# Larger first loads, a reordered start, respaced attention pieces, and the k softmax reciprocal on ScalarE instead of VectorE

## The chip, the cores and the metric

The kernel runs on one core of a Trainium2 chip. The metric is the device time of one execution in microseconds (us). Five engines work side by side, each in the order of its own queue: TensorE (PE, with its weight loads PEld), VectorE (DVE), ScalarE (ACT), GpSimd (POOL) and SyncE (SP, which here only issues transfers).

## The reference

A pre-layernorm block on x of 2048 x 640 (bf16): linear attention with a softmax feature map, then a GELU-gated feed-forward part.

```python
x = A_x
h  = x + A(_layernorm(x), wqkv, w_phi, wo)
h2 = h + (gelu(ln(h) @ w_gate) * (ln(h) @ w_up)) @ w_down        # F = 1536

def A(x, wqkv, w_phi, wo):                                        # 32 heads of 20
    q, k, v = split(x @ wqkv)
    pq, pk = q @ w_phi, k @ w_phi                                 # per head
    phi_q = concat(softmax(pq), softmax(-pq))
    phi_k = concat(softmax(pk), softmax(-pk))
    kv = phi_k^T v;   z = sum over s of phi_k
    o  = (phi_q kv) / (phi_q z + 1e-6)
    return o @ wo
```

## The kernel before

The 2048 rows are 16 tiles of 128 rows, in four blocks of four tiles. Every engine's order is the order of the code: the whole body runs under a manual schedule. SP, too, issues its transfers in code order, and waits at each one for what it reads.

**Start (lines 158 to 196 and 342 to 379).** x tiles 0 to 3 are loaded one by one, alternately from SP and ACT; then ACT loads w_phi, and SP loads Wv in five pieces, x tiles 4 to 7 in two, the transposed k weights WkT, x tiles 8 to 11, WqT, and x tiles 12 to 15. `ln_st` takes the statistics of a tile on DVE (two bn_stats, L106, and one bn_aggr, L108) and the reciprocal root on POOL (L110, L112); with `act=True` POOL also makes mr = -mean*rstd (L117), which `ln_ap` needs when it normalizes on ACT (L123). Otherwise `ln_ap` normalizes on DVE (L128). `ln_tp` transposes a normalized tile on PE into LN1T. `v_part` is a part of a v projection, ordered by weight chunk. `fold` multiplies the k (later q) weights with the block-diagonal feature map BD (L212; BD is built by DVE at L366), and ACT and DVE copy the results to Wk2 (later Wq2) in turn.

**The k loop (lines 384 to 423), one round per tile t.** PE projects k (`k_tile`, L248), ACT makes the two exponentials E of +pk and -pk (L280), PE projects v of tile t+4, ACT copies it to one of six buffers vS (L268). `ln_ap(t + 6)` normalizes a coming tile on ACT, and SP transposes it by a transfer (L139). In `k_norm` DVE sums E by head (L287), takes the reciprocal rs (L291), and v is scaled by it into vt (L295): the half for s = 1 on POOL, the half for s = 0 on DVE one round later, or on POOL for the tiles in VP. At odd t from 5 on, `kv_tile` adds tiles t-5 and t-4 to the kv sums in PSUM (L313). In the last round, t = 15, the first four groups of q (`q_mm`, 35 matmuls of 512 columns, and `q_exp`, their exponentials on ACT, L340) stand in the code between `k_tile(15)` and `k_norm(15)`; kv tiles 10 to 15 follow on PE.

**After the loop.** `kv_mask` brings the sums into the weight KV. PE then takes the rest of q between the attention pieces of tiles 0 and 1, and from there the feed-forward part runs in units: 12 `gate_up` (L556; GELU L559 on ACT, product L562 on DVE) and then `down` (L571). `weave` puts the attention pieces of later tiles ahead of units by hand-written offsets: `attn_a` (L451, L459), `attn_b`, `b2`, `b3` (L472 to L496, and the transposing transfer oT by SP), `attn_c` (L511), `attn_d` (L525), `attn_d2` (L532 to L539), `attn_e` (normalize on ACT, transposing transfer LN2T). Pieces that fall behind the last unit are carried over to the next `weave`. Block 0 is done in two weaves of 256 columns (tiles 0 and 1, then 2 and 3), with 12 gate_up and 4 down units each; the blocks after it are done with 512 columns, and a gate_up of block 1 reads LN2T of all of tiles 4 to 7.

Of the kernel before, what the change touches and what calls it, by code (L numbers as in the profile page):

```python
# [17 lines left out]
def kernel(  # L18
# [74 lines left out]
    def small(pool, shape, name, bufs=3):  # L93
        return pool.tile(shape, F32, name=name, bufs=bufs)
# [1 line left out]
    def gtile(name):  # L96
        return psG.tile([P, 2, 512], F32, name=name, tag="G")

    def ln_stats(pool, tiles, tag, act=True):

        n = len(tiles)
        mv = small(pool, [P, n, nc.vector.BN_AGGR_DIM], "mv" + tag)
        stats = small(pool, [P, n, 2, nc.vector.BN_STATS_DIM], "stats" + tag)
        for j, xt in enumerate(tiles):
            for i in range(2):
                nc.vector.bn_stats(stats[:, j, i, :], xt[:, i * HD:(i + 1) * HD])  # L106
        for j in range(n):
            nc.vector.bn_aggr(mv[:, j, :], stats[:, j])  # L108
        ve = small(pool, [P, n], "ve" + tag)
        nc.gpsimd.tensor_scalar_add(ve, mv[:, :, 1], EPS)  # L110
        rstd = small(pool, [P, n], "rstd" + tag)
        nc.gpsimd.tensor_tensor(rstd, ve, nhalf[:, 0:n], op=ALU.pow)  # L112

        mr = small(pool, [P, n], "mr" + tag)
        if act:
            for j in range(n):
                nc.gpsimd.tensor_scalar(mr[:, j:j + 1], mv[:, j, 0:1], rstd[:, j:j + 1], -1.0,  # L117
                                        op0=ALU.mult, op1=ALU.mult)
        return [(xt, mv[:, j, 0:1], rstd[:, j:j + 1], mr[:, j:j + 1]) for j, xt in enumerate(tiles)]
# [28 lines left out]
    Wk2 = p1.tile([P, NC, D], BF16, name="Wk2")  # L148
    acc = p1.tile([P, NC, 4, VC], F32, name="acc")

    vS = [p1.tile([P, H, VC], BF16, name=f"vS{i}") for i in range(6)]
    fp_cm = tc.tile_pool(name="fp", bufs=1, side="right", reuse_waits="tile")
    fp = fp_cm.__enter__()
    WkT = fp.tile([P, NC, D], BF16, name="WkT")
    WqT = p1.tile([P, NC, D], BF16, name="WqT")


    for t in range(4):
        (nc.sync, nc.scalar)[t % 2].dma_start(x_sb[0][:, t:t + 1, :], x_v[:, t:t + 1, :])
    nc.scalar.dma_start(wphi, phi_v.rearrange("(c p) f -> p c f", p=P))  # L160
    for c in range(NC):
        nc.sync.dma_start(Wv[:, c, :], w_v[:, c, 2 * D:3 * D])
    for t in (0, 2):
        nc.sync.dma_start(x_sb[1][:, t:t + 2, :], x_v[:, 4 + t:6 + t, :])
    nc.sync.dma_start_transpose(WkT, A_wqkv[:, D:2 * D])
    wo_v = A_wo.rearrange("(c p) n -> p c n", p=P)
    wg_v = B_w_gate.rearrange("(c p) n -> p c n", p=P)
# [3 lines left out]
    nc.sync.dma_start(x_sb[3], x_v[:, 12:16, :])  # L171


    nc.gpsimd.memset(nhalf, -0.5)

    ones = fp.tile([P, 2], F32, name="ones")
    nc.scalar.activation(ones, nhalf, ACTF.Exp)
    zero = fp.tile([P, 512], BF16, name="zero")
    nc.vector.memset(zero, 0.0)
    for i in range(6):  # L180
        nc.vector.memset(vS[i][:, :, Dh], 1.0)
    make_identity(nc, ident)
    nc.gpsimd.memset(hmask, 1.0)
# [40 lines left out]

    lnp, Ek, Vt = {}, {}, {}

    def ln_st(*tiles, act=True):
        for t, v in zip(tiles, ln_stats(p1, [x_sb[t // 4][:, t % 4, :] for t in tiles], "1", act)):
            lnp[t] = v

    def ln_ap(t, on_act=False, on_pe=False):
        ln = (ln_act if on_act else ln_dve)(p1, "1", *lnp[t])
        if on_pe:
            lnp[t] = ln
        else:
            transpose_to(LN1T[t // 4][:, :, t % 4 * P:(t % 4 + 1) * P], ln, False)

    def ln_tp(t, on_dve=False):
        transpose_to(LN1T[t // 4][:, :, t % 4 * P:(t % 4 + 1) * P], lnp[t], True, on_dve)
# [18 lines left out]
    def v_part(t, *cs):  # L258

        if 0 in cs:  # L260
            pv[t] = gtile("pv")
        for c in cs:
            for u in range(2):
                nc.tensor.matmul(pv[t][:, u, 0:HD], lhsT=lnT(t, c), rhs=Wv[:, c, u * HD:(u + 1) * HD],
                                 start=(c == 0), stop=(c == NC - 1))

    def v_ev(t):
        nc.scalar.copy(vS[t % 6][:, :, 0:Dh].rearrange("p (u h) f -> p u h f", u=2),  # L268
                       pv[t][:, :, 0:HD].rearrange("p u (h f) -> p u h f", f=Dh))

    def v_tile(t):
        v_mm(t)
        v_ev(t)

    def k_tile(t):
        pk = gtile("pk")
        proj(pk, t, Wk2)
        Ek[t] = ev.tile([P, 2, D], BF16, name="E", bufs=8)
        for s in range(2):
            nc.scalar.activation(Ek[t][:, s, :].rearrange("p (u f) -> p u f", u=2), pk[:, :, 0:HD],  # L280
                                 ACTF.Exp, scale=(1.0 if s == 0 else -1.0))

    def k_norm(t):


        sk = small(p1, [P, 2 * H], "sk")
        nc.vector.reduce_sum(sk, Ek[t].rearrange("p s (h f) -> p (s h) f", f=Dh), axis=AX.X)  # L287
        if t - 1 in todo:
            todo.pop(t - 1)()
        rs = small(p1, [P, 2 * H], "rs")  # L290
        nc.vector.reciprocal(rs, sk)  # L291
        Vt[t] = vt = ev.tile([P, 2, H, VC], BF16, name="vt", bufs=8)

        def mult(s, eng):
            eng.tensor_tensor(vt[:, s], vS[t % 6], rs[:, s * H:(s + 1) * H, None].to_broadcast([P, H, VC]), ALU.mult)  # L295

        mult(1, nc.gpsimd)
        if t in VP:
            mult(0, nc.gpsimd)
        elif t == NT - 1:  # L300
            mult(0, nc.vector)
        else:
            todo[t] = lambda: mult(0, nc.vector)

    todo = {}

    def kv_tile(t):

# [29 lines left out]
    def q_exp(j, signs=(0, 1)):  # L338
        for s in signs:
# [4 lines left out]
    ln_ap(0, on_pe=True)  # L344
    ln_tp(0)
    warm(WA)
    ln_ap(1, on_pe=True)
    ln_tp(1)
    warm(WB)
    ln_st(2, act=False)  # L350
    ln_st(3, act=False)
    ln_ap(2, on_pe=True)
    ln_ap(3, on_pe=True)
    v_part(0, 0, 1, 2)
    v_part(1, 0)
    v_part(0, 3)
    v_part(1, 1)
    ln_tp(2)
    v_part(0, 4)
    v_part(1, 2, 3)  # L360
    ln_tp(3)
    v_part(1, 4)
    v_ev(0)
    v_ev(1)

    nc.vector.tensor_tensor(BD, wphi[:, :, None, :].to_broadcast([P, NC, 8, Dh]),  # L366
                            hmask[:, :, :, None].to_broadcast([P, NC, 8, Dh]), ALU.mult)
    v_tile(2)
    ln_st(4, 5, act=False)
    ln_st(6)  # L370
    v_mm(3, (0,))
    fold(WkT, Wk2, False, (0, 1))
    ln_ap(4, on_pe=True)
# [2 lines left out]
    ln_ap(5, on_pe=True)  # L376
    fold(WkT, Wk2, False, (2, 3, 4))
    ln_tp(4, True)
    ln_st(7)
    fp_cm.__exit__(None, None, None)  # L380
    ev_cm = tc.tile_pool(name="ev", bufs=1, side="right", reuse_waits="tile")
    ev = ev_cm.__enter__()
# [1 line left out]
    for t in range(NT):  # L384
        if t == T3:
            ps_cm.close()
            psG = ps_cm.enter_context(tc.tile_pool(name="psG", bufs=3, space=PSUM, reuse_waits="tile"))
            psK = ps_cm.enter_context(tc.tile_pool(name="psK", bufs=1, space=PSUM, reuse_waits="tile"))
            kvp = psK.tile([P, 2, 512], F32, name="kvp")
        k_tile(t)  # L390
        if t == 0:
            ln_tp(5)
            ln_ap(6)
        if t in FQ:
            fold(WqT, Wq2, True, [i for i, f in enumerate(FQ) if f == t])
        for j in range(len(QT)):
            if t == QT[j]:
                q_mm(j)
                q_exp(j)
        if t + 4 < NT:  # L400
            v_tile(t + 4)
        if t > 0 and t + 6 < NT:
            ln_ap(t + 6, on_act=True)
        if t % 2 == 0 and t + 8 < NT:
            ln_st(t + 8, t + 9)
        k_norm(t)
        if t % 2 == 1 and t >= 5:
            kv_tile(t - 5)
            kv_tile(t - 4)
        if t == 9:  # L410
            nc.gpsimd.memset(KV, 0.0)
            nc.gpsimd.memset(kmask, 1.0)
            for r in HALF:
                nc.gpsimd.affine_select(out=kmask[r], in_=kmask[r], pattern=[[4, NC], [-Dh, 4]],
                                        compare_op=ALU.is_ge, fill=0.0, base=0, channel_multiplier=1)
                nc.gpsimd.affine_select(out=kmask[r], in_=kmask[r], pattern=[[-4, NC], [Dh, 4]],
                                        compare_op=ALU.is_ge, fill=0.0, base=Dh - 1, channel_multiplier=-1)
            nc.gpsimd.tensor_copy(KV[:, :, 0, :, KC - 1], kmask)
            nc.gpsimd.tensor_copy(KV[:, :, 1, :, 0], kmask)
        if t == 10:  # L420
            nc.sync.dma_start(Wg, wg_v)
            nc.sync.dma_start(Wo, wo_v)
            nc.sync.dma_start(Wu, wu_v)
# [181 lines left out]
    def gus(b, a0, a1):  # L605
        return [(gate_up, b, f, a0, a1) for f in range(NF)]
# [33 lines left out]
    attn_e(0, True, True)  # L640
    q_mm(q + 6)
    q_exp(q + 6)
    attn_ln(1, True)
    attn_e(1, True, True)
    attn_a(2, 2)
# [2 lines left out]
    def attn_at(t, i, offs):  # L648
# [2 lines left out]
        return [(i + o, fn, t) for fn, o in zip(fns, offs) if o >= 0]  # L651

    SHORT = (0, 2, 3, 4, 9, 9, 10, 12)
    LONG = (0, 1, 2, 3, 6, 6, 7, 8)


    weave(gus(0, 0, 256) + downs(0, (0, 1)),
          attn_at(2, 0, (-1, 0, 1, 2, 7, 7, 8, 10)) + attn_at(3, 1, SHORT) + attn_at(4, 6, SHORT) + attn_at(5, 9, SHORT) +
          attn_at(6, 13, SHORT))
    weave(gus(0, 256, 512) + downs(0, (2, 3)), attn_at(7, 2, SHORT))  # L660
    for b in range(1, NB):
        stages = []
        if b + 1 < NB:
# [34 lines left out]
```

The softmax here doesn't subtract the row's maximum and nothing guards it: scores larger than these inputs give would overflow.

## Time and profile before

| | us |
|---|---|
| median of 12 runs | 283.61 (283.44 to 284.79) |
| the profiled execution: time | 283.56 |
| its span in the profile | 281.8 |
| PE busy / DVE / ACT / POOL | 272.8 / 166.1 / 140.3 / 95.6 |
| first projection of v starts (PE) | 7.90 |
| first projection of k starts (PE) | 16.66 |
| q groups in round 15, first start (PE) | 62.09 |
| last kv sum ends (PE) | 72.22 |
| first gate_up of block 1 starts (PE) | 146.24 |

The profile gives all times in us from the span's start; the execution's own time is 1.76 us more than the span. "PE busy" counts overlapping matmuls once and is near to the span; where PE waits is read from the chain of waits and from the order of its instructions. The transposing transfers appear as instructions of SP (SPq) where they are issued, with their landing told apart.

### The profile page before, as it was taken

How to read it: one execution, taken by the hardware profiler on the slowest of the kernel's cores; microseconds unless marked ns; L12 is line 12 of the kernel's file. 1: busy time of each engine (PE TensorE's matmuls, PEld its weight loads, DVE VectorE, ACT ScalarE, POOL GpSimd, SP SyncE). 2: the span in 40 equal slices, each digit the busy share in tenths (PEclk: the TensorE clock that was granted, in tenths of full speed). 3: DMA queues.
4: the chain of work that ended last, by engine and by line, in shares of the span. 5: the costliest groups of instructions: out<-in, count | busy, mean ns of one | idle time of the engine just before them, and what ended most of it. 6: DMA issues, size and time to landing. Idle time of an engine off the chain costs nothing.

```text
span 281.8 us, 5752 instructions
## 1 busy us (share of the span) xinstructions
PE 272.8 (97%) x2326; PEld 171.5 (61%) x2326; DVE 166.1 (59%) x289; ACT 140.3 (50%) x226; POOL 95.6 (34%) x211
## 2 busy tenths in 40 slices
PE   7999999999999999999799999999999999999995
PEld 2677777764555777778564555675455567444573
DVE  4999998788496676667223848332566632333222
ACT  2679889678596855465334454412446350222200
POOL 6258987686102217436112234210135230000000
PEclk9999999999999999999999999999999999999999
DMA  7991332693520021322120113131031613000011
GB/s 223 256 267 29 72 45 53 181 392 129 185 99 0 3 47 34 84 49 59 38 68 4 23 27 70 25 95 47 2 47 23 70 27 93 26 0 1 0 49 47
DMA packets 40523, 21.05 MB, mean 75 GB/s; under 512 B 33200, under 2 KB 38704, under 8 KB 40496
## 3 DMA queue, kind: packets, MB, share of 16 engines
q1 hardware_dynamic: 39552, 20.32, 28.5%
q10 hardware_dynamic: 944, 0.35, 0.5%
q8 instruction: 18, 0.29, 0.5%
q14 instruction: 9, 0.07, 0.1%
HBM read 10.18 MB, written 2.62 MB: 45 GB/s over the span
## 4 chain that ended last, share of the span: by engine, by line
PE 86%; DVE 5%; ACT 3%; DMA 3%; POOL 1%; issue 1%; ACTq 0%; POOLq 0%
PE gu L556 35%; PE pd L571 18%; PE pq L335 8%; PE po L511 7%; PE pk L248 7%; PE pv L248 5%; PE kvp L313 2%; PE ab L451 2%; DVE stats L106 2%; DMA oT<-o 2%; DMA x_sb<-in_A_x_dram 1%; DVE sk L287 1%; ACT E L280 1%; ACT Eq L340 1%; PE wa L212 1%
## 5 line engine op out<-in xcount | busy, mean ns | idle before, releaser
L559 ACT ACTIVATE g<-gu 128x512 bf16<-128x512 f32 (+1 forms) x60 | 30.7, 512 | 75.2 <-PE gu L556 74.0
L562 DVE TENSOR_TENSOR GT<-gu,g 128x512 bf16<-128x512 f32 (+1 forms) x60 | 34.5, 581 | 54.2 <-ACT g L559 54.0
L556 PE MATMUL gu<-LN2T,Wg 128*128 128x512 bf16 (+1 forms) x300 | 61.8, 337 | 0.9 <-DVE GT L562 0.8
L556 PE MATMUL gu<-LN2T,Wu 128*128 128x512 bf16 (+1 forms) x300 | 61.7, 336 | 0.0
L571 PE MATMUL pd<-Wd,GT 128*128 128x320 bf16 x384 | 53.9, 299 | 0.0
L571 PEld LDWEIGHTS <-GT 128*128 128x128 bf16 x384 | 37.4, 98 | 15.7 <-DVE GT L562 0.9
L556 PEld LDWEIGHTS <-Wu 128*128 128x128 bf16 x300 | 29.3, 98 | 22.6
L556 PEld LDWEIGHTS <-Wg 128*128 128x128 bf16 x300 | 28.4, 98 | 21.7 <-issue 1.0
L248 PEld LDWEIGHTS <-LN1T 128*128 128x128 bf16 x300 | 28.5, 98 | 11.6 <-issue 0.7
L295 POOL TENSOR_TENSOR vt<-vS,rs 128x672 bf16<-128x672 bf16 x22 | 29.8, 1372 | 9.1 <-DVE rs L291 7.1
L577 DVE TENSOR_TENSOR y<-pd,x_sb 128x640 bf16<-128x640 f32 (+1 forms) x17 | 13.3, 784 | 30.7 <-PE pd L571 30.7
L459 ACT COPY AB<-ab 128x704 f32<-128x704 f32 x28 | 19.6, 748 | 14.4 <-PE ab L451 14.1
L511 PE MATMUL po<-Wo,oT 128*128 128x320 bf16 x160 | 24.4, 299 | 1.8 <-DMA oT<-o 1.8
L287 DVE TENSOR_REDUCE sk<-E 128x64 f32<-128x1280 bf16 x16 | 23.3, 1455 | 3.3 <-ACT E L280 3.3
L248 PE MATMUL pk<-Wk,LN1T 128*128 128x320 bf16 x160 | 24.1, 299 | 0.4 <-ACT E L280 0.3
L492 DVE TENSOR_TENSOR tt<-AB,w 128x1280 bf16<-128x1280 f32 x16 | 23.8, 1487 | 1.2 <-POOL w L485 0.9
L280 ACT ACTIVATE E<-pk 128x640 bf16<-128x640 f32 x32 | 20.8, 706 | 6.8 <-PE pk L248 6.6
L335 PE MATMUL pq<-LN1T,Wq 128*128 128x512 bf16 x100 | 22.9, 379 | 0.0
L248 PE MATMUL pv<-Wv,LN1T 128*128 128x320 bf16 x140 | 21.3, 299 | 0.0
L340 ACT ACTIVATE Eq<-pq 128x1024 bf16<-128x1024 f32 (+1 forms) x22 | 19.4, 950 | 3.7 <-PE pq L335 3.7
L511 PEld LDWEIGHTS <-oT 128*128 128x128 bf16 x160 | 15.5, 98 | 9.2 <-DMA oT<-o 2.2
L534 POOL TENSOR_SCALAR v<-sm 128x1 f32<-128x1 f32 x14 | 8.4, 599 | 32.0 <-DVE x_sb L525 32.0
(80 smaller groups left out, 262.5 us busy)
## 6 DMA issues: line engine op xcount, KB each, us to landing
out_dram<-y SPq DMA_DIRECT2D x15, 160.0 KB, 1.9
Wg<-in_B_w_gate_dram SPq DMA_DIRECT2D x1, 1920.0 KB, 7.5
Wu<-in_B_w_up_dram SPq DMA_DIRECT2D x1, 1920.0 KB, 14.9
Wd<-in_B_w_down_dram SPq DMA_DIRECT2D x1, 1920.0 KB, 7.8
x_sb<-in_A_x_dram SPq DMA_DIRECT2D x2, 640.0 KB, 4.7
Wv<-in_A_wqkv_dram SPq DMA_DIRECT2D x5, 160.0 KB, 3.9
Wo<-in_A_wo_dram SPq DMA_DIRECT2D x1, 800.0 KB, 9.1
x_sb<-in_A_x_dram SPq DMA_DIRECT2D x2, 320.0 KB, 4.7
```

Of the source, the lines that this page charges most:

```text
L248: nc.tensor.matmul(ps[:, u, 0:HD], lhsT=lnT(t, c), rhs=W[:, c, u * HD:(u + 1) * HD], start=(c == 0), stop=(c == NC - 1))
L280: nc.scalar.activation(Ek[t][:, s, :].rearrange("p (u f) -> p u f", u=2), pk[:, :, 0:HD], ACTF.Exp, scale=(1.0 if s == 0 else -1.0))
L287: nc.vector.reduce_sum(sk, Ek[t].rearrange("p s (h f) -> p (s h) f", f=Dh), axis=AX.X)
L295: eng.tensor_tensor(vt[:, s], vS[t % 6], rs[:, s * H:(s + 1) * H, None].to_broadcast([P, H, VC]), ALU.mult)
L335: nc.tensor.matmul(pqs[j][:, i, :], lhsT=Wq2[:, kc, c * P:(c + 1) * P], rhs=LN1T[b][:, kc, :], start=(kc == 0), stop=(kc == NC - 1))
L340: nc.scalar.activation(Eq[j][:, :, s, :], pqs[j][:, 0:len(QG[j])], ACTF.Exp, scale=(1.0, -1.0)[s])
L492: nc.vector.tensor_tensor(tt.rearrange("p s (h f) -> p s h f", f=Dh), num, w[:, :, :, None].to_broadcast([P, 2, H, Dh]), ALU.mult)
L511: nc.tensor.matmul(po[:, u, 0:HD], lhsT=st[t][:, c, :], rhs=Wo[:, c, u * HD:(u + 1) * HD], start=(c == 0), stop=(c == NC - 1))
L556: nc.tensor.matmul(gu[:, i, 0:n], lhsT=W[:, c, f * P:(f + 1) * P], rhs=LN2T[b][:, c, a0:a1], start=(c == 0), stop=(c == NC - 1))
L559: nc.scalar.activation(g[:, 0:n], gu[:, 0, 0:n], ACTF.Gelu_apprx_tanh)
L562: nc.vector.tensor_tensor(st[b, "g", f][:, a0:a1], gu[:, 1, 0:n], g[:, 0:n], ALU.mult)
L571: nc.tensor.matmul(pd[:, u, 0:HD], lhsT=st[b, "g", f][:, tl * P:(tl + 1) * P], rhs=Wd[:, f, u * HD:(u + 1) * HD], start=(f == 0), stop=(f ...
```

## The change

First loads: x tile 0 from SP, tile 1 from ACT, tiles 2 and 3 in one load from SP; Wv in three loads; of tiles 4 to 7 one half from SP, one from ACT. An explicit load of activation table set 6 replaces the small Exp that came first on ACT. Start: the normalizing of tile 1 goes between the two bn_stats of tile 2; BD is built ahead of the normalizing of tile 3; the v parts of tiles 0 and 1 stand in another order. k loop: `ln_ap(t + 6)` on DVE; E is summed in two halves; Ln and Exp(-x) on ACT (`k_rs`) give the reciprocal, one round later; `k_vt` makes both halves of vt after it; vS has seven buffers. In round 15 `k_rs(15)` and `k_vt(15)` follow at once. After the loop a small GELU stands behind the last q_exp. Attention pieces: from `attn_c` on, tiles 4 to 6 come one unit later; tile 7 starts one unit later, and its `attn_c` and the pieces after it come two later.

```diff
-    def ln_stats(pool, tiles, tag, act=True):
+    def ln_stats(pool, tiles, tag, act=True, between=None):
...
                 nc.vector.bn_stats(stats[:, j, i, :], xt[:, i * HD:(i + 1) * HD])
+                if between and i == j == 0:
+                    between()
...
-    for t in range(4):
-        (nc.sync, nc.scalar)[t % 2].dma_start(x_sb[0][:, t:t + 1, :], x_v[:, t:t + 1, :])
+    nc.gpsimd.memset(nhalf, -0.5)
+    nc.sync.dma_start(x_sb[0][:, 0:1, :], x_v[:, 0:1, :])
+    nc.scalar.dma_start(x_sb[0][:, 1:2, :], x_v[:, 1:2, :])
+    nc.sync.dma_start(x_sb[0][:, 2:4, :], x_v[:, 2:4, :])
+    for c0, c1 in ((0, 2), (2, 4), (4, 5)):
+        nc.sync.dma_start(Wv[:, c0:c1, :], w_v[:, c0:c1, 2 * D:3 * D])
+
+    nc.scalar.add_instruction(mybir.InstLoadActFuncSet(name=nc.get_next_instruction_name(), act_func_set_id=6))
     nc.scalar.dma_start(wphi, phi_v.rearrange("(c p) f -> p c f", p=P))
-    for c in range(NC):
-        nc.sync.dma_start(Wv[:, c, :], w_v[:, c, 2 * D:3 * D])
-    for t in (0, 2):
-        nc.sync.dma_start(x_sb[1][:, t:t + 2, :], x_v[:, 4 + t:6 + t, :])
+    nc.sync.dma_start(x_sb[1][:, 0:2, :], x_v[:, 4:6, :])
+    nc.scalar.dma_start(x_sb[1][:, 2:4, :], x_v[:, 6:8, :])
     nc.sync.dma_start_transpose(WkT, A_wqkv[:, D:2 * D])
...
-    nc.gpsimd.memset(nhalf, -0.5)
-
-    ones = fp.tile([P, 2], F32, name="ones")
-    nc.scalar.activation(ones, nhalf, ACTF.Exp)
...
-    for i in range(6):
+    for i in range(7):
         nc.vector.memset(vS[i][:, :, Dh], 1.0)
...
             nc.scalar.activation(Ek[t][:, s, :].rearrange("p (u f) -> p u f", u=2), pk[:, :, 0:HD],
                                  ACTF.Exp, scale=(1.0 if s == 0 else -1.0))
+        if t > 0:
+            k_rs(t - 1)
+
+    def k_rs(t):
+
+        sk = st1[t]
+        nc.scalar.activation(sk, sk, ACTF.Ln)
+        st1[t] = rs = small(p1, [P, 2 * H], "rs")
+        nc.scalar.activation(rs, sk, ACTF.Exp, scale=-1.0)
...
     def k_norm(t):
-        sk = small(p1, [P, 2 * H], "sk")
-        nc.vector.reduce_sum(sk, Ek[t].rearrange("p s (h f) -> p (s h) f", f=Dh), axis=AX.X)
-        if t - 1 in todo:
-            todo.pop(t - 1)()
-        rs = small(p1, [P, 2 * H], "rs")
-        nc.vector.reciprocal(rs, sk)
+        st1[t] = sk = small(p1, [P, 2 * H], "sk")
+        for s in range(2):
+            nc.vector.reduce_sum(sk[:, s * H:(s + 1) * H], Ek[t][:, s, :].rearrange("p (h f) -> p h f", f=Dh), axis=AX.X)
+
+    def k_vt(t):
+
+        rs = st1[t]
         Vt[t] = vt = ev.tile([P, 2, H, VC], BF16, name="vt", bufs=8)
...
+        for s in (1, 0):
+            eng = nc.gpsimd if s == 1 or t in VP else nc.vector
+            eng.tensor_tensor(vt[:, s], vS[t % 7], rs[:, s * H:(s + 1) * H, None].to_broadcast([P, H, VC]), ALU.mult)
...
-    ln_ap(1, on_pe=True)
+    ln_st(2, act=False, between=lambda: ln_ap(1, on_pe=True))
     ln_tp(1)
     warm(WB)
-    ln_st(2, act=False)
     ln_st(3, act=False)
     ln_ap(2, on_pe=True)
+
+    nc.vector.tensor_tensor(BD, wphi[:, :, None, :].to_broadcast([P, NC, 8, Dh]),
+                            hmask[:, :, :, None].to_broadcast([P, NC, 8, Dh]), ALU.mult)
     ln_ap(3, on_pe=True)
-    v_part(0, 0, 1, 2)
-    v_part(1, 0)
-    v_part(0, 3)
-    v_part(1, 1)
+    v_part(0, 0, 1, 2, 3, 4)
+    v_part(1, 0, 1)
     ln_tp(2)
-    v_part(0, 4)
-    v_part(1, 2, 3)
+    v_part(1, 2, 3, 4)
     ln_tp(3)
-    v_part(1, 4)
     v_ev(0)
     v_ev(1)
-
-    nc.vector.tensor_tensor(BD, wphi[:, :, None, :].to_broadcast([P, NC, 8, Dh]),
-                            hmask[:, :, :, None].to_broadcast([P, NC, 8, Dh]), ALU.mult)
     v_tile(2)
     ln_st(4, 5, act=False)
-    ln_st(6)
+    ln_st(6, act=False)
...
         if t > 0 and t + 6 < NT:
-            ln_ap(t + 6, on_act=True)
+            ln_ap(t + 6)
         if t % 2 == 0 and t + 8 < NT:
-            ln_st(t + 8, t + 9)
+            ln_st(t + 8, t + 9, act=False)
         k_norm(t)
+        if t > 0:
+            k_vt(t - 1)
+        if t == NT - 1:
+            k_rs(t)
+            k_vt(t)
...
     q_mm(q + 6)
     q_exp(q + 6)
+
+    dummy = small(p2, [P, 2], "dummy", 1)
+    nc.scalar.activation(dummy, nhalf, ACTF.Gelu_apprx_tanh)
...
     SHORT = (0, 2, 3, 4, 9, 9, 10, 12)
+    SHORT2 = (0, 2, 3, 4, 10, 10, 11, 13)
...
-          attn_at(2, 0, (-1, 0, 1, 2, 7, 7, 8, 10)) + attn_at(3, 1, SHORT) + attn_at(4, 6, SHORT) + attn_at(5, 9, SHORT) +
-          attn_at(6, 13, SHORT))
-    weave(gus(0, 256, 512) + downs(0, (2, 3)), attn_at(7, 2, SHORT))
+          attn_at(2, 0, (-1, 0, 1, 2, 7, 7, 8, 10)) + attn_at(3, 1, SHORT) + attn_at(4, 6, SHORT2) + attn_at(5, 9, SHORT2) +
+          attn_at(6, 13, SHORT2))
+    weave(gus(0, 256, 512) + downs(0, (2, 3)), attn_at(7, 3, SHORT2))
```

More of the change, by code (lines that the diff above doesn't have):

```diff
@@ L149 @@
     acc = p1.tile([P, NC, 4, VC], F32, name="acc")
-    vS = [p1.tile([P, H, VC], BF16, name=f"vS{i}") for i in range(6)]
+    vS = [p1.tile([P, H, VC], BF16, name=f"vS{i}") for i in range(7)]
     fp_cm = tc.tile_pool(name="fp", bufs=1, side="right", reuse_waits="tile")
@@ L225, with ln_st @@
     lnp, Ek, Vt = {}, {}, {}
-    def ln_st(*tiles, act=True):
-        for t, v in zip(tiles, ln_stats(p1, [x_sb[t // 4][:, t % 4, :] for t in tiles], "1", act)):
+    def ln_st(*tiles, act=True, between=None):
+        for t, v in zip(tiles, ln_stats(p1, [x_sb[t // 4][:, t % 4, :] for t in tiles], "1", act, between)):
             lnp[t] = v
@@ L267, in v_ev @@
     def v_ev(t):
-        nc.scalar.copy(vS[t % 6][:, :, 0:Dh].rearrange("p (u h) f -> p u h f", u=2),
+        nc.scalar.copy(vS[t % 7][:, :, 0:Dh].rearrange("p (u h) f -> p u h f", u=2),
                        pv[t][:, :, 0:HD].rearrange("p u (h f) -> p u h f", f=Dh))
@@ L281, in k_tile @@
                                  ACTF.Exp, scale=(1.0 if s == 0 else -1.0))
-    def k_norm(t):
-        sk = small(p1, [P, 2 * H], "sk")
-        nc.vector.reduce_sum(sk, Ek[t].rearrange("p s (h f) -> p (s h) f", f=Dh), axis=AX.X)
-        if t - 1 in todo:
-            todo.pop(t - 1)()
-        rs = small(p1, [P, 2 * H], "rs")
-        nc.vector.reciprocal(rs, sk)
-        Vt[t] = vt = ev.tile([P, 2, H, VC], BF16, name="vt", bufs=8)
[L294 to L305, printed above, removed]
+        if t > 0:
[5 more added lines that the diff above has]
+        nc.scalar.activation(rs, sk, ACTF.Exp, scale=-1.0)
+    st1 = {}
+    def k_norm(t):
+        st1[t] = sk = small(p1, [P, 2 * H], "sk")
[3 more added lines that the diff above has]
+        rs = st1[t]
+        Vt[t] = vt = ev.tile([P, 2, H, VC], BF16, name="vt", bufs=8)
+        for s in (1, 0):
+            eng = nc.gpsimd if s == 1 or t in VP else nc.vector
+            eng.tensor_tensor(vt[:, s], vS[t % 7], rs[:, s * H:(s + 1) * H, None].to_broadcast([P, H, VC]), ALU.mult)
     def kv_tile(t):
@@ L378 @@
     ln_tp(4, True)
-    ln_st(7)
+    ln_st(7, act=False)
     fp_cm.__exit__(None, None, None)
```

## The prediction

> **What bounds the kernel now.** I read the busy shares first (PE 97% of the span, DVE 59%, ACT 50%), then the chain of waits, and then the timeline at each place where the chain leaves PE. From 16.66 us on the chain is PE in almost every piece, so a change is worth what it adds to or takes from PE's waits, and the 16.66 us ahead of that. Four places matter. The first two, from the chain (start, length, what):
>
> ```profile
> 15.32 0.70 ACT vS L268
> 16.02 0.60 ACT Wk L221
> 16.62 0.04 issue
> 16.66 1.57 PE pk L248 x10
> ...
> 29.36 0.82 ACT ln L123
> 30.18 1.20 ACT E L280 x2
> 31.38 0.04 issue
> 31.42 1.52 PE pk L248 x10
> ...
> 69.80 2.42 PE kvp L313 x120
> 72.22 2.27 PE pq L335 x10
> ```
>
> The first k projection waits for ACT, which evicts v of tile 3 and then weights. At 31.42 PE waits for ACT again: the normalizing of a coming tile (`ln`, 0.92 us each) stands ahead of E. From 31.42 to 72.22 no other engine appears: this stretch has no wait to gain. The third place is round 15 (timeline: start, length, engine, line):
>
> ```profile
> 68.76 2.92 ACT L340 ACTIVATE Eq<-pq 128x1024 bf16<-128x1024 f32 x4 [0.22 <-PE pq L335]
> 68.78 0.86 DVE L295 TENSOR_TENSOR vt<-vS,rs 128x672 bf16<-128x672 bf16 x1
> 68.85 1.97 POOL L295 TENSOR_TENSOR vt<-vS,rs 128x672 bf16<-128x672 bf16 x1 [1.35 <-PE pq L335]
> 69.73 2.49 PE L313 MATMUL kvp<-vt,E 128*64 128x84 bf16 x120
> ```
>
> vt of tile 15 is ready at 70.82 (68.85+1.97); kv of tile 15, last of the six, starts at 69.80+5*0.40=71.8. The spare is 1.0 us. ACT ends its q exponentials only at 71.68. The fourth place is the attention of tile 7:
>
> ```profile
> 132.30 1.20 SPq L139 DMA_TRANSPOSE oT<-o  x1
> 136.67 1.53 PE L511 MATMUL po<-Wo,oT 128*128 128x320 bf16 x10 [1.77 <-DMA oT<-o]
> 142.85 1.20 SPq L139 DMA_TRANSPOSE LN2T<-ln  x1
> 146.24 1.25 PE L556 MATMUL gu<-LN2T,Wg 128*128 128x512 bf16 x5
> ```
>
> PE waits 1.77 us for oT of tile 7, which took 4.3 us to land instead of the usual 2.6. LN2T of tile 7 lands at 142.85+2.6=145.45, only 0.8 us before block 1 reads it.
>
> **What the Trainium skill says.** "ScalarE: Activation LUTs", Table sets: exp and ln share one set, natural_log_exp_and_others, so Ln next to Exp needs no switch; the trace has two table loads of 1283 ns, one ahead of the first Exp, one ahead of the first GELU, and no load between functions of a set. "SBUF — State Buffer", SBUF: two separate sides: DVE and GpSimd share a port pair by an exclusive lock. The trace agrees: the last POOL vt, beside a DVE vt, took 1.97 us, the median one 1.315. "DMA: Bandwidth & Descriptors", Issuing engines are not separate DMA queues: issuing from a second engine saves only issue time; here an issue takes 0.4 to 0.6 us.
>
> **The change, part by part.**
>
> *First loads.* x0 and x1 are issued at 0.79 as before, so the first statistics stay at 3.81. Three issues fewer on SP (two of Wv, one x load) bring WkT some 1.5 us forward from 6.42. Its landing (6.42+6.6=13.0) was ahead of its reader (13.68), so nothing follows. The table load moves from 2.21 to about 1.3 on ACT and holds w_phi and half of tiles 4 to 7 behind it by 1.28; w_phi is then issued at 2.5 and lands by 7.2 (4.7 us to land), its reader BD runs at about 9.7. The small Exp (0.20) goes; ACT was idle there until 6.94. The seventh memset (0.13) lies in DVE's wait for x0. Sum 0.
>
> *Start.* DVE had 0.72 of idle time until rstd of tile 1 at 7.11; one bn_stats of tile 2 (0.44) now fits in it. Tile 2's normalizing ends at 9.68 instead of 10.06. PE does 14 v matmuls before tp2 (12 before); it waited 0.3 for the copy of LN1T of tile 1 and 0.29 for ln2, and five chunks of tile 0 first (10*0.136=1.36 from 7.90) cover the first wait. So tp2 comes at 9.8 for 10.12. BD (0.98) ahead of ln3 leaves ln3 where it was: 9.68+0.98+0.45=11.1, before 11.01. All of v0 and v1 are then done, so `v_tile(2)` starts at 11.1+0.3=11.4 for 11.78. The eviction of tile 3 on ACT and the chain to pk follow: **-0.35**. Bounds: 0 (ACT's evictions of v0 to v2, which follow tp3, bind) and -0.8 (BD is gone from DVE's path to tiles 4 and 5).
>
> *The k loop.* Per round ACT loses 0.92 (ln) for nine tiles and gains Ln and Exp on 128x64. No such row exists; between 203 ns for 128x2 and 706 for 128x640 lies 250 each (the same page's 186+0.833*64 gives 239, in agreement), so +0.5. DVE loses the reciprocal (0.55), gains 0.06 for the second reduce and 0.44 for ln: level. POOL loses the mr (0.25 to 0.5 a tile). E of tile 4 is then ready at 30.3 in the old clock, before PE wants the buffer, and the wait at 31.42 goes: PE work from 21.07 is seven projections (7*1.36) and a fold (0.32), which ends at 30.9 to 31.06. **-0.35**, bounds -0.5 and, for the new coupling, +2: Ln waits on ACT for DVE's sums, and behind it stand v's eviction and the next E, whose PSUM buffers PE needs. I lay DVE's queue out with these durations: its sums end about 0.5 after E in rounds 5 and 7 and in time elsewhere; ACT has 0.4 to 0.7 of spare per round, so I take 0.
>
> *Round 15.* `k_rs(15)` stands behind all four q_exp in ACT's queue. With everything 0.7 earlier, ACT is done with them at 71.68-0.70=70.98, the pair takes 0.5, vt starts on POOL and DVE together at 71.5, and POOL's half, beside DVE's, takes 1.97: 73.5, and the s = 1 half of kv 15 (0.2) ends at 73.7. Without a wait it would end at 72.22-0.70=71.52. PE waits **+2.2**. The mask chain follows and hides under the next q group as before (2.26 of PE work). Nothing later gives it back: PE has no wait from there to 91.3. Bounds: +1.5 (POOL at 1.31) and +2.5.
>
> *The small GELU.* The table load already runs at once behind the last q_exp (93.31, when the exponentials end at 93.29), and the first GELU at 94.61 is what PE waits for. The dummy adds one 128x2 ACTIVATE: **+0.2**.
>
> *Respacing.* Tile 4's `attn_c` moves behind the last down unit, which it only swaps with. Tile 5's moves behind the third gate_up, so DVE's products of the first units are out in time and the 0.46 wait at 123.55 goes. Tile 7: `b3` now stands behind `attn_d(6)`; oT is issued at about 133.1 in the old clock and lands at 135.7 (2.6) or 137.4 (4.3); `attn_c` stands behind one more gate_up and a down (1.65) and starts at 137.0. So the waits of 0.46 and 1.8 go. But then only three downs (4.95) and one ab (0.5) stand between po of tile 7 (137.0 to 138.4) and block 1, and the path to LN2T takes 138.4 + 0.2 + x add 0.9 + square 0.95 + POOL 1.35 + normalize 0.95 + landing 2.6 = 145.4. PE arrives at 143.8 and waits 1.6. Block 1 starts at 145.4 for 146.24: **-0.8**. Bounds: -1.0 and, should such a slow landing (4.6 us was seen once for LN2T) fall on this transfer, +1.2.
>
> **Sum:** -0.35-0.35+2.2+0.2-0.8 = +0.9, on the profiled execution's 283.56 (span 281.8 and 1.76 around it). That execution is 0.05 under the median, so the median becomes 283.61+0.9, about **284.5 us**.
>
> **Rivals.**
>
> 1. *Faster: the last reciprocal isn't late.* If ACT reaches Ln and Exp of tile 15 ahead of the q exponentials, so that rs is there by about 69.1 (71.1 when kv 15 is due, less 1.97), the +2.2 is gone and the sum is -1.3: 282.3. For it: the sums of tile 15 were ready at 67.4 before. Against: ACT kept the order of the code everywhere in the trace.
> 2. *No change:* the wait is only 1.5 (POOL undisturbed) and the start gives up to 0.8: +0.9-0.7-0.45 = -0.25, about 283.4.
> 3. *Slower, coupling:* four odd rounds in which Ln waits 0.5 for DVE, each passed on to PE: +0.9+2.0 = 286.5. For it: DVE is busy 14.37 of the 14.76 us from 16.66 to 31.42. Against: PE's buffers had room later.
> 4. *Slower, a slow landing on LN2T of tile 7:* +0.9+2.0 = 286.5.
> 5. *Not what it says:* the tables are switched between Ln and Exp after all, 32 loads of 1.28 = 41 us on ACT, some 30 of them on PE's path.
>
> **How the numbers follow.** About 0.2% (0.57 us) is what a measurement of this kernel can tell from no change. The forecast (284.0 to 285.3) has 0.48, most of it slower, a part at its low end within 0.2%; rival 1 has 0.14, rival 2 0.13, rivals 3 and 4 together 0.22, rival 5 0.03. Faster: 0.15. Within 0.2%: 0.2. Slower: 0.65. The range 282.9 to 286.5 leaves out most of rivals 1 and 5 and the far end of 3.
>
> **What would show it.** The first pk at 16.3; no wait of PE for E near 31; ACT rows for Ln and Exp of 0.25; a PE wait of about 2 us for vt (POOL) ahead of the last kv matmuls; the first GELU 0.2 after the table load ends; no wait for oT of tile 7, but one of about 1.6 for LN2T before block 1. The forecast fails if the last kv starts without a wait, if PE waits in rounds 4 to 9 for ACT, or if the start gains over 1 us.

## The result: slower by 2%

The changed kernel takes 289.38 us (median of 8 runs, 288.75 to 290.58), the kernel before 283.66 us in the runs beside it. The ratio is 1.0203, 95% interval 1.019 to 1.0217: 5.7 us slower. The forecast was 284.5 us in a range of 282.9 to 286.5. The direction was right, the size was not.

The profiled execution took 289.16 us (span 287.4), 5.6 us more span than before. Reading the same landmarks in both profiles shows in which stretch they lie:

| stretch (us) | before | after | difference | forecast |
|---|---|---|---|---|
| start to the first k projection | 16.66 | 16.99 | +0.33 | -0.35 |
| k loop: from there to the first q group of round 15 | 45.59 | 49.54 | +3.95 | -0.35 |
| round 15: from there to the end of the kv sums | 9.97 | 12.41 | +2.44 | +2.2 |
| the rest | 209.58 | 208.46 | -1.12 | -0.6 |

The chain of waits after (start, length, what) around the stretches that the prediction showed:

```profile
16.34 0.60 ACT Wk L223
16.95 0.04 issue
16.99 1.57 PE pk L250 x10
...
36.15 1.76 DVE vt L308
37.91 0.73 DVE Wq L225
38.64 0.62 DVE ln L130
...
46.78 1.52 PE pk L250 x10
...
76.52 2.00 POOL vt L308
78.52 0.04 issue
78.56 0.38 PE kvp L317 x10
78.94 2.26 PE pq L339 x10
```

Before, the chain was PE from 31.42 on. Now it runs through DVE, piece after piece, from 26.6 to 46.7 us: DVE has become the engine that sets the pace of the k loop. The two windows from the first pk to the first q group, before and then after (columns: length, then busy us of PE, PEld, DVE, ACT and POOL with the number of instructions in brackets, then the granted clock of PE, the DMA share and GB/s) say the same:

```profile
16.66:62.25 45.59, 45.31 (x516) 32.98 (x516) 41.70 (x66) 36.94 (x56) 36.02 (x46) 1.00 0.51 134
```

```profile
16.99:66.53 49.54, 45.49 (x516) 33.25 (x516) 47.05 (x76) 34.75 (x74) 32.66 (x37) 1.00 0.44 131
```

PE's work is the same. DVE's busy time rose by 5.35 us, to more than PE's. These are PE's waits in the loop after (total us, times, longest us; before, the only one listed there was 0.3 us for E):

```profile
PE pk L250 <- DVE Wq L225: 2.8, 2, 1.8
PE wa L214 <- ACT Wq L223: 1.1, 1, 1.1
PE pk L250 <- ACT Wk L223: 0.2, 1, 0.2
```

Two waits for weights that DVE evicts, and one for weights that ACT evicts behind an Ln that had itself waited 1.64 us for DVE's sums, make up 3.9 us: all of them go back to DVE. The timeline after shows how the longest one comes about:

```profile
34.91 0.22 POOL L112 TENSOR_SCALAR ve<-mv 128x2 f32<-128x2 f32 x1 [2.55 <-DVE mv L110]
35.21 0.71 POOL L114 TENSOR_TENSOR rstd<-ve,nhalf 128x2 f32<-128x2 f32 x1
35.88 4.56 POOL L308 TENSOR_TENSOR vt<-vS,rs 128x672 bf16<-128x672 bf16 x3
36.15 1.76 DVE L308 TENSOR_TENSOR vt<-vS,rs 128x672 bf16<-128x672 bf16 x1
37.83 0.81 DVE L225 CAST Wq<-wa 128x640 bf16<-128x640 f32 x1
38.70 1.52 PE L250 MATMUL pk<-Wk,LN1T 128*128 128x320 bf16 x10 [1.84 <-DVE Wq L225]
```

POOL sat 2.55 us waiting for DVE's statistics, with vt queued behind them; then its vt of tile 3 and DVE's half of the same tile start 0.27 us apart. DVE's takes 1.76 us instead of 0.85. The weight eviction behind it is late by that, so 0.9 of the 1.84 us that PE waits for its PSUM buffer come from this one pair. The rows of vt, before and then after (minimum, median and maximum in ns, first and last start in us):

```profile
L295 DVE TENSOR_TENSOR vt<-vS,rs x10: 847/855/940, 27.7 to 68.8; 128x672 bf16<-128x672 bf16 x10
```

```profile
L308 DVE TENSOR_TENSOR vt<-vS,rs x10: 842/1638/1789, 28.0 to 76.5; 128x672 bf16<-128x672 bf16 x10
L130 DVE TENSOR_SCALAR ln<-x_sb,mv,rstd x18: 393/446/1433, 6.2 to 97.2; 128x640 bf16<-128x640 bf16 x18
```

DVE's normalizing, 0.44 us alone, also takes up to 1.43 beside POOL's vt (0.63 in the mean in the loop).

### The profile page after: what moved, and what is told of

It reads as the page before. It is cut to its first block, busy times and chain, and to the rows that moved or that the text cites. A ratio compares the mean times of both kernels' runs of the same rounds, so it can differ in the third digit from the quotient of the medians.

```text
span 287.4 us, 5757 instructions
## 1 busy us (share of the span) xinstructions
PE 273.2 (95%) x2326; PEld 172.0 (60%) x2326; DVE 170.3 (59%) x299; ACT 138.5 (48%) x249; POOL 95.7 (33%) x201
## 4 chain that ended last, share of the span: by engine, by line
PE 81%; DVE 8%; ACT 4%; DMA 2%; issue 2%; POOL 2%; POOLq 0%; ACTq 0%
PE gu L560 36%; PE pd L575 17%; PE po L515 8%; PE pq L339 7%; PE pk L250 5%; PE pv L250 4%; DVE sk L300 2%; PE ab L455 2%; DVE stats L106 2%; ACT Eq L344 2%; DVE ln L130 1%; DMA x_sb<-in_A_x_dram 1%; PE kvp L317 1%; DMA LN2T<-ln 1%; DVE vt L308 1%
## 5 line engine op out<-in xcount | busy, mean ns | idle before, releaser
L308 POOL TENSOR_TENSOR vt<-vS,rs 128x672 bf16<-128x672 bf16 x22 | 32.5, 1499 | 12.9 <-ACT rs L292 12.8
L300 DVE TENSOR_REDUCE sk<-E 128x32 f32<-128x640 bf16 x32 | 24.4, 804 | 2.5 <-ACT E L282 2.4
L125 ACT ACTIVATE ln<-x_sb,v,rstd 128x640 bf16<-128x640 bf16 x14 | 12.9, 920 | 12.4 <-POOL v L543 12.2
```

What stands on the lines that cost most here:

```text
L300: nc.vector.reduce_sum(sk[:, s * H:(s + 1) * H], Ek[t][:, s, :].rearrange("p (h f) -> p h f", f=Dh), axis=AX.X)
L308: eng.tensor_tensor(vt[:, s], vS[t % 7], rs[:, s * H:(s + 1) * H, None].to_broadcast([P, H, VC]), ALU.mult)
```

## The experiments

Theory after the result: in the loop DVE loses time to POOL (two engines that block each other), because the change makes both halves of vt ready by one instruction of ACT and puts the normalizing on DVE as well; round 15 loses by the order on ACT. Rivals: the changed loads of the start disturb the loop; DVE is merely too full; the gain after the loop comes from elsewhere.

The stretch from the first pk to the first q group, and the median DVE vt, in one profiled execution of each kernel:

| kernel | time, median us | first pk | loop | DVE vt, ns |
|---|---|---|---|---|
| before | 283.5 to 283.8 | 16.7 | 45.4 | 855 |
| after | 289.38 | 17.0 | 49.4 | 1638 |
| k_undone | 282.64 | 16.8 | 46.0 | 855 |
| stagger | 287.7 | 16.6 | 48.2 | 1478 |
| rcp15 | 286.41 | 16.7 | 49.4 | 1636 |
| ln_act | 286.49 | 16.5 | 46.3 | 1076 |
| pool_first | 286.24 | 17.3 | 46.8 | 1076 |
| respace | 283.03 | 16.6 | 45.9 | 854 |
| best, again | 280.4, 280.65 | 16.0, 16.3 | 45.4, 45.9 | 854, 849 |
| k_mended | 281.44 | 16.0 | 46.5 | 1634 |

(Here the loop runs from the first start of a pk to the first start of a q matmul, to 0.1 us. The tables above take the q group from the chain of waits, where it comes 0.1 to 0.2 us later, so their figures are larger by that. respace has the loop of the kernel before unchanged and took 45.9 us, so a difference of 0.5 us between two profiles says little.)

**k_undone: everything but the k part.**

```diff
-        if t > 0:
-            k_rs(t - 1)
...
-        for s in range(2):
-            nc.vector.reduce_sum(sk[:, s * H:(s + 1) * H], Ek[t][:, s, :].rearrange("p (h f) -> p h f", f=Dh), axis=AX.X)
+        nc.vector.reduce_sum(sk, Ek[t].rearrange("p s (h f) -> p (s h) f", f=Dh), axis=AX.X)
+        if t - 1 in todo:
+            todo.pop(t - 1)()
+        rs = small(p1, [P, 2 * H], "rs")
+        nc.vector.reciprocal(rs, sk)
...
-            ln_ap(t + 6)
+            ln_ap(t + 6, on_act=True)
-            ln_st(t + 8, t + 9, act=False)
+            ln_st(t + 8, t + 9)
-        if t > 0:
-            k_vt(t - 1)
-        if t == NT - 1:
-            k_rs(t)
-            k_vt(t)
```

The lines left out at the dots put the scaling of v, `ln_st(7)` and `todo` back to what they were.

> The changed kernel with its k softmax put back (one sum, DVE's reciprocal, normalizing in the loop on ACT, DVE's half of vt one round late); loads, start, small GELU and respacing stay. Theory (the loss is the k part: DVE and POOL block each other in the loop, 3.9 us, and the last reciprocal is late, 2.4 us): the first pk stays at about 17.0, the last kv sum ends at about 72.5, and the time is 283.66 + 0.33 (start) - 1.12 (after the loop) = 282.9 us. Rival (the changed loads and transposes of the start disturb the loop): the loop stays 2 us or more too long, 285 to 289 us.

Measured: 282.64 us, ratio to the kernel before 0.9971 (0.9961 to 0.9981). The k part alone makes the loss, 6.7 us: the profiled executions are 6.0 us apart, of which 3.4 lie in the loop, 2.4 in round 15 (back at 9.97) and 0.2 ahead of the first pk. What is left of the change is a small gain. The rival of the loads falls.

**rcp15: the last reciprocal on DVE.**

```diff
-            k_rs(t)
+            sk = st1[t]
+            st1[t] = rs = small(p1, [P, 2 * H], "rs")
+            nc.vector.reciprocal(rs, sk)
             k_vt(t)
```

> The changed kernel with the reciprocal of tile 15 alone on DVE, so that it no longer stands behind the four q exponentials on ACT. Theory: PE's wait for vt of tile 15 (1.27 for DVE's half, 0.79 for POOL's) goes, the rest stays: 287.1 to 287.4 us. Rival (the wait only moves on, to the mask chain or the next q group): 288.5 us or more.

Measured: 286.41 us, 3.0 below the changed kernel; in the profiles the span is 2.7 shorter, 0.3 of it ahead of the first pk. PE's waits for vt are gone. After, these were the lines of round 15:

```profile
73.04 2.92 ACT L344 ACTIVATE Eq<-pq 128x1024 bf16<-128x1024 f32 x4 [0.22 <-PE pq L339]
76.19 0.26 ACT L292 ACTIVATE rs<-sk 128x64 f32<-128x64 f32 x1
76.48 0.86 DVE L308 TENSOR_TENSOR vt<-vS,rs 128x672 bf16<-128x672 bf16 x1 [4.49 <-ACT rs L292]
76.52 1.99 POOL L308 TENSOR_TENSOR vt<-vS,rs 128x672 bf16<-128x672 bf16 x1 [5.58 <-ACT rs L292]
78.56 0.38 PE L317 MATMUL kvp<-vt,E 128*64 128x84 bf16 x10 [0.79 <-POOL vt L308]
```

The reciprocal stands behind the q exponentials that end at 75.96, and two engines idle 4.5 and 5.6 us for it. That is the place, the cause and nearly the price that the prediction gave.

**stagger: DVE's half one round later, ahead of DVE's sums.**

```diff
+        if t - 2 in todo:
+            todo.pop(t - 2)()
         k_norm(t)
...
         if t == NT - 1:
+            if t - 1 in todo:
+                todo.pop(t - 1)()
             k_rs(t)
```

`todo` holds DVE's half of vt of each tile that has one; `k_vt`, left out here, fills it.

> The changed kernel with DVE's half of vt one round later than POOL's, ahead of DVE's sums, as the two no longer become ready by the same instruction of ACT. Theory (DVE waits[...] in those pairs): the mean DVE vt falls from 1.47 us to about 0.9, some 6 us of DVE time in the loop, most of PE's 3.9 us of waits go, and the time is about 286.4 us. Rival (DVE is simply full since it has the normalizing as well, or Ln on ACT waits for the sums in any order): DVE's vt gets shorter, PE's waits stay, 288.5 to 289.5 us.

Measured: 287.7 us, ratio 1.0166 (1.0136 to 1.0196): 1.7 below the changed kernel and 1.3 above what was expected. It tells less than it should, because the collision stayed: the median DVE vt is still 1.48 us, the mean 1.43 where 0.9 was expected. DVE's half met another of POOL's (one of 1.96 us at 36.89 lies within three of POOL's from 35.48 to 40.03).

**pool_first: only POOL's order changed.**

```diff
+        if t > 0:
+            k_vt(t - 1)
         if t % 2 == 0 and t + 8 < NT:
             ln_st(t + 8, t + 9, act=False)
         k_norm(t)
         if t > 0:
-            k_vt(t - 1)
+            k_vt0(t - 1)
...
             k_vt(t)
+            k_vt0(t)
```

`k_vt` is here the half for s = 1, on POOL; `k_vt0` the half for s = 0, on DVE or, for tiles in VP, on POOL.

> The changed kernel with one thing reordered, on POOL alone: in each round POOL's half of vt of tile t-1 stands ahead of the reciprocal roots of tiles t+8 and t+9, which wait for DVE's statistics; DVE's queue is unchanged. Theory (DVE's half of vt is blocked because POOL's half of the same tile, held back by that reciprocal root, starts beside it): the mean DVE vt falls from 1.47 us to about 1.0, the stretch from the first pk to the first q group from 49.4 to about 47 us, and the time to about 287 us. Rival (DVE is full with the normalizing in any case): DVE's vt may fall, the stretch stays above 48.8 us, the time at 288.6 to 289.4 us.

Measured: 286.24 us, ratio 1.0078 (1.0047 to 1.0109), 3.1 below the changed kernel, and the loop 2.6 shorter (its first q group comes 2.3 earlier, as the first pk of this execution was 0.3 later). The same place as above:

```profile
32.78 1.31 POOL L313 TENSOR_TENSOR vt<-vS,rs 128x672 bf16<-128x672 bf16 x1 [0.94 <-ACT rs L292]
...
34.69 0.71 POOL L114 TENSOR_TENSOR rstd<-ve,nhalf 128x2 f32<-128x2 f32 x1
...
35.63 0.85 DVE L313 TENSOR_TENSOR vt<-vS,rs 128x672 bf16<-128x672 bf16 x1
...
37.26 1.52 PE L250 MATMUL pk<-Wk,LN1T 128*128 128x320 bf16 x10 [0.93 <-DVE Wq L225]
```

POOL's vt of tile 3 is over at 34.09, before DVE's begins; DVE's takes 0.85 us, and PE's wait is 0.93 instead of 1.84. DVE's instructions and their order are those of the changed kernel, so time that DVE gains here it had lost to POOL working beside it: over the ten vt the mean falls from 1.47 to 1.18 us, and two thirds of the loop's loss go with that. The collisions are fewer, not gone: 1.0 was expected, and the longest vt is still 1.78.

**ln_act: the normalizing back on ACT.**

```diff
-    ln_st(7, act=False)
+    ln_st(7)
...
-            ln_ap(t + 6)
+            ln_ap(t + 6, on_act=True)
-            ln_st(t + 8, t + 9, act=False)
+            ln_st(t + 8, t + 9)
```

> The changed kernel with the normalizing in the loop put back on ACT, mr on POOL again. Theory (both DVE's vt and its normalizing lose time[...], and DVE's sums are late for Ln by that): DVE loses 9 pieces of 0.55 us, PE's waits of 3.9 us fall by 1.5 to 3, 286.5 to 288 us. Rival (the pairs of vt alone are the cause): within 0.5 us of 289.4.

Measured: 286.49 us, with a wide interval of the ratio, 1.0068 to 1.0148 (the four runs lie in two pairs, at 285.5 and at 287.4 to 287.8; the profiled one is of the first); the loop is 3.1 shorter in the profile. DVE's vt are still slow (mean 1.26 us), but with nine pieces fewer DVE has room for that: PE waits for no eviction of DVE's, and Ln never waits for DVE's sums. So it takes both for the loss: DVE filled up by the normalizing, and its operations lengthened by POOL. With one of the two taken away, here or in pool_first, 0.9 to 1.4 us of the loop's loss is left. Here it is of another kind, one wait of PE of 0.8 us for an LN1T transfer (see k_mended).

**respace: only the attention pieces of tiles 4 to 7, on the kernel before.**

```diff
-          attn_at(2, 0, (-1, 0, 1, 2, 7, 7, 8, 10)) + attn_at(3, 1, SHORT) + attn_at(4, 6, SHORT) + attn_at(5, 9, SHORT) +
-          attn_at(6, 13, SHORT))
-    weave(gus(0, 256, 512) + downs(0, (2, 3)), attn_at(7, 2, SHORT))
+          attn_at(2, 0, (-1, 0, 1, 2, 7, 7, 8, 10)) + attn_at(3, 1, SHORT) + attn_at(4, 6, SHORT2) + attn_at(5, 9, SHORT2) +
+          attn_at(6, 13, SHORT2))
+    weave(gus(0, 256, 512) + downs(0, (2, 3)), attn_at(7, 3, SHORT2))
```

> The kernel before with the respacing of the attention pieces of tiles 4 to 7 alone. Theory (what was gained after the loop is the respacing, 1.1 us, less 0.2 lost by the small GELU): 282.3 to 282.7 us, with a wait of 1.4 us for LN2T of tile 7 ahead of block 1 and none for oT. Rival (the gain of k_undone comes from the start): within 0.3 us of the kernel before.

Measured: 283.03 us, ratio 0.997 (0.9961 to 0.9978): 0.8 us, about all that k_undone gained, and 0.3 us short of the expected range. As forecast, the wait for oT goes and one for LN2T of tile 7 comes, 1.6 us.

**best: the good parts, mended.** Against k_undone:

```diff
+    ln_ap(3, on_pe=True)
     nc.vector.tensor_tensor(BD, wphi[:, :, None, :].to_broadcast([P, NC, 8, Dh]),
                             hmask[:, :, :, None].to_broadcast([P, NC, 8, Dh]), ALU.mult)
-    ln_ap(3, on_pe=True)
...
-    dummy = small(p2, [P, 2], "dummy", 1)
-    nc.scalar.activation(dummy, nhalf, ACTF.Gelu_apprx_tanh)
...
-    weave(gus(0, 256, 512) + downs(0, (2, 3)), attn_at(7, 3, SHORT2))
+    weave(gus(0, 256, 512) + downs(0, (2, 3)), attn_at(7, 2, SHORT2))
```

> k_undone without the small GELU, with BD built behind the normalizing of tile 3 again, and with tile 7's pieces one unit earlier (its attn_b3 then stands ahead of attn_d of tile 6 on DVE, its attn_c ahead of the first down unit). Theory: POOL's reciprocal root of tile 3 falls from 1.42 to 0.57 us beside no BD, the first pk comes 0.3 to 0.5 earlier; the first GELU 0.1 to 0.2 earlier; the wait of 1.4 us for LN2T of tile 7 goes: 282.64 - 0.4 - 0.15 - 1.3 = 280.8 us. Rival (the wait for LN2T turns into one for oT of tile 7, or DVE's order hurts the products): 282 to 282.6 us.

> The same kernel as best, on the same chip as k_mended: 280.2 to 280.7 us.

Measured: 280.4 and 280.65 us, ratios to the kernel before 0.9871 (0.9837 to 0.9906) and 0.9886 (0.9859 to 0.9912). It beats both kernels by over 3 us. The three edits have no runs of their own; two readings of the profile say what two of them do. BD beside POOL's reciprocal root of tile 3, after and then in best:

```profile
9.87 1.41 POOL L114 TENSOR_TENSOR rstd<-ve,nhalf 128x1 f32<-128x1 f32 x1
9.88 0.97 DVE L357 TENSOR_TENSOR BD<-wphi,hmask 128x800 bf16<-128x800 bf16 x1
```

```profile
9.40 0.56 POOL L114 TENSOR_TENSOR rstd<-ve,nhalf 128x1 f32<-128x1 f32 x1
...
10.36 0.99 DVE L355 TENSOR_TENSOR BD<-wphi,hmask 128x800 bf16<-128x800 bf16 x1
```

One element per lane took 1.41 us because BD ran beside it. And block 1, after and then in best:

```profile
143.77 1.52 PE L515 MATMUL po<-Wo,oT 128*128 128x320 bf16 x10
...
152.06 1.25 PE L560 MATMUL gu<-LN2T,Wg 128*128 128x512 bf16 x5 [1.38 <-DMA LN2T<-ln]
```

```profile
134.65 1.52 PE L507 MATMUL po<-Wo,oT 128*128 128x320 bf16 x10
...
143.12 1.25 PE L552 MATMUL gu<-LN2T,Wg 128*128 128x512 bf16 x5
```

After, block 1 could start 8.3 us after po of tile 7, the last 1.38 of them a wait. With po of tile 7 ahead of all four down units PE has 8.5 us of work in between, and it waits no more.

**k_mended: is the reciprocal on ACT worth anything in a better order?** It has the edits of pool_first, ln_act, rcp15 and best together; against best it comes to this:

```diff
+        if t > 0:
+            k_rs(t - 1)
...
-        nc.vector.reciprocal(rs, sk)
...
         if t > 0 and t + 6 < NT:
             ln_ap(t + 6, on_act=True)
+        if t > 0:
+            k_vt(t - 1)
...
         k_norm(t)
+        if t > 0:
+            k_vt0(t - 1)
```

> Ln and Exp on ACT kept for tiles 0 to 14, with all that the runs so far speak for: POOL's half of vt ahead of the reciprocal roots, the normalizing in the loop on ACT, tile 15's reciprocal on DVE, no small GELU, BD behind tile 3's normalizing, tile 7 as in best. Theory (the k part lost time only by the collisions and by the order in round 15; the loop is bound by PE at about 45.3 us from the first pk to the first q group either way, so the reciprocal on ACT is worth nothing by itself): within 0.4 us of best, about 280.4. Rival (Ln's wait for DVE's sums costs in any order): 281.2 us or more. Rival (it frees DVE and PE gains): 279.9 or less.

Measured: 281.44 us, ratio 0.9916 (0.989 to 0.9943), 0.8 to 1.0 us above best. In this order the reciprocal on ACT costs rather than gains. The number is the first rival's, its reason is not: Ln never waits for DVE's sums here. The trace shows what does cost (DVE's vt, then the chain of waits around the only wait of PE listed in the loop):

```profile
L313 DVE TENSOR_TENSOR vt<-vS,rs x10: 844/1634/1995, 26.2 to 68.7; 128x672 bf16<-128x672 bf16 x10
```

```profile
22.44 0.68 ACT vS L270
23.12 0.81 ACT ln L125
23.96 3.10 DMA LN1T<-ln
27.05 0.05 issue
27.10 1.53 PE pv L250 x10
```

The collisions are all still there, the vt as slow as in the changed kernel, for DVE is now in time and its half begins 0.4 us after POOL's. Yet PE waits for nothing of DVE's: the collision alone, on a DVE that has room, costs PE no wait in this loop. What PE waits for, 0.90 us, is one LN1T transfer. From the projection of k ahead of it, the normalizing on ACT begins 1.05 us later here (21.96 to 23.01) and 0.79 in best (21.80 to 22.59), as Ln and Exp now stand ahead of it; and the transfer takes 3.10 us instead of 2.58. ln_act has the same wait, with 3.01. Why the transfer is longer in these two isn't known, and part of the wait may be spread: respace and k_undone, without Ln on ACT, have one such wait of 0.4 and 0.6 us, behind a transfer of 3.35 and 3.64 us. As the collisions stayed, no run shows what the reciprocal on ACT would be worth without them.

## Why the prediction was wrong

- **First loads: +0 was right.** x0 landed 3.28 us after its issue, 2.99 before; but in the other kernels with the same loads it took 2.81 to 3.22, so the 0.3 is spread from run to run. The step that ACT's transfers wait behind the table load was wrong: they were issued at 1.25 and 1.72 while the load ran from 1.22 to 2.50. It cost nothing either way.
- **Start: -0.35 failed at one term.** Up to tile 2 it went as worked out (tp2 at 10.09, of which 0.28 is x0's landing, v matmuls without a gap). But "ln3 at 11.1" took POOL's reciprocal root at 0.57; beside BD it was 1.41, and ln3 ended at 11.77. With BD behind it (best, best_again), the first pk comes 0.4 to 0.6 us earlier than before, counted from the landing of x0: about what was estimated, once the collision is away.
- **The k loop: the failing step.** The working said of DVE "level" and of the new coupling "I take 0". The counts were right: Ln and Exp took 258 and 256 ns against 250, the second reduce and the normalizing about what was put in. Wrong were the durations: DVE's vt was taken at its old 0.85, and was 1.47 in the mean, 6 us over ten; the normalizing was taken at 0.44 and was 0.63 in the mean in the loop, at most 1.43. So DVE was not level but busy for 47.05 us where it had been for 41.70, and the loop grew by 3.95 us where -0.35 was forecast. It took both: with vt still slow but the normalizing on ACT (ln_act, k_mended) PE no longer waits for DVE in the loop. The prediction itself cited from the Trainium skill ("SBUF — State Buffer", SBUF: two separate sides) that DVE and POOL share a port pair by an exclusive lock, and used it in round 15 alone; in the loop the trace agrees as well, with 1.76 us for a DVE vt that begins 0.27 us after POOL's. It didn't ask what had kept the two apart in the loop before: DVE itself made the reciprocal, behind its own half of the tile before, so POOL couldn't start the next half until DVE was done with that one (DVE's vt before: 940 ns at most). The change takes that order away. This reading of the old order is argued from the code; that POOL's work beside DVE costs the time is shown by pool_first, for the part that it takes away.
- **Rival 3** had the direction, Ln waiting for late sums, but at 0.5 us a round from the undisturbed durations. After, ACT waited 1.64 and 0.67 for the sums, which passed 1.1 us on to PE; the larger part, 2.8 us of PE's waits, was for DVE's own weight evictions, which the rival didn't name.
- **Round 15: +2.2 was right** (2.44 in the profile, and rcp15 takes it away), by the steps given, down to POOL's 1.99 beside DVE.
- **The small GELU: +0.2 was right in kind.** It ran 0.20 us at 101.33, behind the table load; counted from the start of that load, DVE's product of the first GELU began 1.80 us later, before 1.71, so 0.1 rather than 0.2. No run has it alone.
- **Respacing: -0.8** was right in sum (0.8 gained by respace, which has it alone) and in both waits; PE's wait for LN2T was 1.4 to 1.6.

Put together: with +0.3 for the start and +3.95 for the loop in place of -0.35 each, the sum becomes +5.9 instead of +0.9, against 5.7 measured.

## What to carry to other kernels

When an operation moves from one engine to another, ask which order it enforced by standing where it did. Here, as far as the code tells, a reciprocal on DVE kept DVE and POOL from working on vt at the same time; moved to ACT, it released both at once. And before adding work to an engine that is nearly full (DVE was busy 41.70 of 45.59 us here), price its operations as they run beside the neighbour that they will meet, not as they ran alone. A longer operation costs nothing as long as its engine has room, as k_mended shows. Last, a result that is needed at the end of a stage must not be queued behind the next stage's bulk work.

## What the runs showed of the hardware

- Ln and Exp on 128x64 f32 on ACT take 258 and 256 ns, and no table load came between them: after has two loads, one at 1.22 us and one ahead of the first GELU.
- A DVE operation beside POOL's vt took up to 1.79 us in the changed kernel and 1.99 in k_mended (vt, alone 0.85) or 1.43 (normalizing, alone 0.44), while DVE's sums of E kept 1.49 to 1.55 us a pair. POOL suffers too: 0.57 became 1.41 beside BD, and its vt 1.99 for 1.31 in round 15. In these pairs the one that begins later is the long one: DVE's vt 0.27 us behind POOL's took 1.76, POOL's 0.04 behind DVE's took 1.99 (DVE's then 0.86), and POOL's reciprocal root 0.2 behind BD took 1.19 (rcp15). For the root of 1.41 the starts, 9.87 and 9.88, are too near to each other to say which came first.
- A transposing transfer that usually lands in 2.4 to 2.7 us sometimes takes 3.0 to 4.7 (4.3 for oT of tile 7 before, 4.1 for one LN1T in best_again, 3.10 for the one that PE waits for in k_mended). The cause was not found.
